# Two column halves instead of four column strips in the last matmuls of a decode layer, and its output stored as four rows

## The chip, the cores and the metric

The kernel runs on one core of a Trainium2 chip. The metric is the time of one execution on the device in microseconds (us), as the median of several runs. A separate execution is recorded by the hardware profiler; its span, from the first instruction to the last, is a little shorter than the time of that execution, because something lies around it.

A core has five engines that run side by side and meet through semaphores: TensorE (PE, the matmuls; its weight loads are shown apart as PEld), VectorE (DVE), ScalarE (ACT), GpSimd (POOL) and SyncE (SP), which here only issues DMAs. Matmuls write to PSUM, which has 128 partitions and eight banks of 512 fp32 columns; VectorE and ScalarE copy the results from there to SBUF, and DMAs move data between SBUF and the main memory (HBM).

## The reference

One decode step of a layer for B = 4 sequences with D = 512: attention over the last W = 4096 positions of a key and value cache (32 query heads, 8 key heads, 128 wide) in parallel with a gated feed-forward block (F = 1792), both on the same normalised input.

```python
xn  = layernorm(x)                                  # 4 x 512
q   = xn @ wq                                       # 32 heads of 128
p   = softmax(q @ k[last 4096].T * 128 ** -0.5)
att = (p @ v[last 4096]) @ wo
ffn = (silu(xn @ w_gate) * (xn @ w_up)) @ w_down
out = x + att + ffn                                 # 4 x 512, bf16
```

All tensors are bf16. The caches of the window are 64 MB, the weights some 13 MB.

## The kernel before

**The stream.** SP issues all the large loads from one queue, in the order of their use (`run_sync`, L227): W_q, the two feed-forward weights, then for each of the eight key heads 4 MB of keys and 4 MB of values into two buffers each, W_down, and W_o in five pieces (`ROWS`: rows j 0 to 15, 16 to 21, 22 to 28, 29 and 30, and 31), each piece with a semaphore of its own. Each load waits until the buffer that it fills is free.

**The start.** GpSimd writes constants (`run_gpsimd`, L190): identities, selection matrices, and `Dsh`, whose rows 64 to 67 hold 0 where a column belongs to a sequence and -BIG elsewhere. They come from a fill with zeros (L192), a fill of the four rows with -BIG (L209) and an `affine_select` (L211), which keeps an element where the compare holds and writes `fill` elsewhere. After the last constant it gives `s_const` (L220), for which PE (ahead of L461) and VectorE (ahead of L303) wait; then it fills P, guT and OP (L221 to L223). Meanwhile VectorE makes the layer norm, PE the projections with W_q (L467) and the feed-forward inputs (L481).

**The heads.** For each key head PE transposes the keys (L415), forms the scores (L424), the sums of exponentials (L515) and the product with the values (L433); VectorE and ScalarE copy, take maxima and exponentials in between. All that is not touched by the change.

**The end.** In `t_tail` (L554 on) PE gathers the heads' outputs, and accumulates in one PSUM bank, `part_ps`, the product with W_down (L566) and that with the first 22 rows of W_o (`EARLY`, L574). Row j stands for the 128 rows of W_o with index p * 32 + j; its weights on PE are `OP[:, j, :]`, 128 x 32. Each matmul there has 512 columns and goes to one of four strips of 32 partitions, so the four strips hold four partial sums of the whole output. VectorE copies partitions 0 to 63 of it to SBUF (L390), ScalarE partitions 64 to 127 (L274).

Then the order of the work turns round: in `acc_ps`, one bank, each strip n of 32 partitions holds the columns 128 n to 128 n + 127 of the output. First `fold`, a matrix of ones and zeros, sums the four partial sums (L579, fp32, one matmul a strip); then the last ten rows of W_o are added (L586, four matmuls of 128 columns for each row j, one a strip), each piece after a wait for its load. The last matmul gives `s_acc`; VectorE casts the 128 x 128 block to bf16 (L392) and gives `s_y`; SP stores it (L254) and waits for the store (L255). Only every eighth partition of a strip holds a sequence, so the store reads 16 partitions (`y_ap`), 256 bytes of each, into a pattern of three levels in HBM (`out_ap`). GpSimd waits for `s_acc` at its end (L225); nothing waits for that.

Of the kernel before, what the change touches and what calls it, by code (L numbers as in the profile page):

```python
# [3 lines left out]
BF16 = mybir.dt.bfloat16  # L4
FP32 = mybir.dt.float32
ALU = mybir.AluOpType
# [4 lines left out]
def bass_parallel_sum__sliding_block_cached__swiglu_ffn__decode_kernel(  # L11
# [12 lines left out]
    B, _, D = A_x.shape  # L24
# [11 lines left out]
    NC = D // 128  # L36
    NF = F // 128
    REP = HQ // HKV
# [6 lines left out]
    BIG = 1.0e30  # L45
# [3 lines left out]
    sb = nc.alloc_sbuf_tensor  # L49
# [6 lines left out]
    WO = KB[0][:].rearrange("p t d -> p (t d)").rearrange("p (j n) -> p j n", n=D)  # L56
# [22 lines left out]
    Dsh = sb("dsh", [128, CQ], BF16)  # L79
# [5 lines left out]
    OP = sb("oP", [128, 32, 32], BF16)  # L85
    guT = sb("guT", [128, NF, 32], BF16)
    part = sb("part", [128, D], FP32)
    y = sb("y_sb", [128, 128], BF16)

    ident = sb("ident", [128, 128], BF16)  # L90
    identf = sb("identf", [128, 128], FP32)
# [3 lines left out]
    fold = sb("fold", [128, 32], FP32)  # L95
# [6 lines left out]
    ps_S = [ps("ps_s%d" % s, [128, 512], FP32) for s in range(NB)]  # L102
# [14 lines left out]
    part_ps = ps_S[0]  # L117
    rt_ps = kt_ps[0][:, 0, :]
    op_ps = ps_S[1][:].rearrange("p (b q j) -> p b q j", b=B, q=4)
    acc_ps = ps_S[2]  # L120

    def sem(name):
        return nc.alloc_semaphore(name=name)
# [46 lines left out]
    s_acc = sem("s_acc")  # L170
    s_y = sem("s_y")

    x_ap = A_x.rearrange("b s d -> (b s) d")
    out_ap = out.rearrange("b s (n c) -> n (b s) c", n=NC)
    y_ap = y[0:128:8, :]
    wq_ap = A_wq.rearrange("(p c) n -> p c n", c=NC)
    wg_ap = B_w_gate.rearrange("(p c) n -> p c n", c=NC)
    wu_ap = B_w_up.rearrange("(p c) n -> p c n", c=NC)
# [11 lines left out]
    def run_gpsimd(eng):  # L190
        for t in (ident, identf, I4w, I48, Lsel, sel, mxd, Dsh):
            eng.memset(t[:], 0.0)  # L192
        eng.memset(ones[:], 1.0)
        eng.drain()
        eng.affine_select(ident[:], ident[:], pattern=[[-1, 128]], compare_op=ALU.not_equal,
                          fill=1.0, base=0, channel_multiplier=1).then_inc(s_c2, 1)
        eng.affine_select(identf[:], identf[:], pattern=[[-1, 128]], compare_op=ALU.not_equal,
                          fill=1.0, base=0, channel_multiplier=1)
        eng.drain()
        eng.memset(Lsel[0:16, :], 1.0)  # L200
        eng.drain()
        eng.memset(Lsel[32:48, :], 1.0)
        eng.drain()
        eng.affine_select(Lsel[64:68, :].rearrange("k (s b) -> k s b", b=B),
                          Lsel[64:68, :].rearrange("k (s b) -> k s b", b=B),
                          pattern=[[0, 32], [-1, B]], compare_op=ALU.not_equal,
                          fill=1.0, base=0, channel_multiplier=1)
        eng.drain()
        eng.memset(Dsh[64:68, :], -BIG)  # L209
        eng.drain()  # L210
        eng.affine_select(Dsh[64:68, :].rearrange("k (b h) -> k b h", b=B),  # L211
                          Dsh[64:68, :].rearrange("k (b h) -> k b h", b=B),
                          pattern=[[-1, B], [0, REP]], compare_op=ALU.not_equal,
                          fill=0.0, base=0, channel_multiplier=1)
        eng.drain()
        for q in range(4):
            v = sel[:].rearrange("k b (r h e) -> k b r h e", r=HKV, h=REP)[:, :, :, :, q]
            eng.affine_select(v, v, pattern=[[-REP, B], [-CQ, HKV], [-1, REP]], compare_op=ALU.not_equal,
                              fill=1.0, base=0, channel_multiplier=1)
        eng.drain().then_inc(s_const, 1)  # L220
        eng.memset(P[:], 1.0)  # L221
        eng.memset(guT[:], 0.0)
        eng.memset(OP[:], 0.0)  # L223
        eng.drain().then_inc(s_fill, 1)
        eng.wait_ge(s_acc, 1)  # L225

    def run_sync(eng):  # L227
        def load_k(r):
            if r >= 2:
                eng.wait_ge(s_tr[NCH - 1], r - 1)  # L230
            eng.dma_start(KB[r % 2][:].rearrange("p t d -> p (t d)"), kv_ap(A_k_cache, r)).then_inc(d_k[r % 2], 16)

        def load_v(r):
            if r:
                eng.wait_ge(s_pv, r)
            eng.dma_start(VB[r % 2][:].rearrange("p t d -> p (t d)"), kv_ap(A_v_cache, r)).then_inc(d_v[r % 2], 16)

        eng.dma_start(WQ[:], wq_ap).then_inc(d_v[1], 16)
        eng.dma_start(WG[:], wg_ap).then_inc(d_wg, 16)
        eng.dma_start(WU[:], wu_ap).then_inc(d_wu, 16)  # L240
        load_k(0)
        load_k(1)
        load_v(0)
        for r in range(2, HKV):
            load_k(r)
            load_v(r - 1)
        load_v(HKV - 1)
        eng.dma_start(WD, wd_ap).then_inc(d_wd, 16)  # L248
        for q, (a, b) in enumerate(ROWS):
            if q == 0:  # L250
                eng.wait_ge(s_tr[NCH - 1], HKV - 1)
            eng.dma_start(WO[:, a:b, :], wo_ap[:, a:b, :]).then_inc(d_wo[q], 16)  # L252
        eng.wait_ge(s_y, 1)
        eng.dma_start(out_ap, y_ap).then_inc(d_out, 16)  # L254
        eng.wait_ge(d_out, 16)  # L255

    def run_scalar(eng):
        eng.dma_start(X[:], x_ap).then_inc(d_x, 16)
        eng.wait_ge(s_var, 1)
        eng.activation(st_std[:], st_var[:], ACT.Sqrt).then_inc(s_std, 1)  # L260
        eng.wait_ge(s_q, 1)
        eng.copy(qs[:, 1, :], ps_S[1][:]).then_inc(s_qs, 1)
        eng.wait_ge(s_g, 1)
        eng.activation(ex, gate_ps[:], ACT.Exp, scale=-1.0).then_inc(s_ex, 1)
        with eng.Fori(0, HKV) as i:
            for n in BY_ACT:
                eng.wait_ge(s_tr[n], i + 1)
                eng.copy(KT[n % 8][:], kt_ps[n % 3]).then_inc(s_ev[n], 1)  # L268
            for q in range(NB):
                eng.wait_ge(s_sh[q], i + 1)  # L270
                eng.activation(P[:, q * TB:(q + 1) * TB, :], S_ps[q], ACT.Exp,  # L271
                               scale=SCALE).then_inc(s_xp[q], 1)
        eng.wait_ge(s_pt, 1)
        eng.copy(part[64:128, :], part_ps[64:128, :]).then_inc(s_ptc, 1)  # L274

    def run_vector(eng):
        me = bass.OrderedEngineSet([eng.engine])
# [111 lines left out]
        eng.wait_ge(s_pt, 1)  # L389
        eng.tensor_copy(part[0:64, :], part_ps[0:64, :]).then_inc(s_ptc, 1)  # L390
        eng.wait_ge(s_acc, 1)
        eng.tensor_copy(y[:], acc_ps[:, 0:128]).then_inc(s_y, 1)  # L392

    def run_tensor(eng):
        mm = eng.matmul
# [54 lines left out]
        with nc.body("t_head", valid_engines=me):  # L450
# [13 lines left out]
            for c in range(NC):  # L464
                for j in range(2):
                    for k in range(4):
                        last = mm(ps_S[j][32 * k:32 * k + 32, :], XnT[:, c, :],  # L467
                                  WQ[:, c, 512 * (4 * j + k):512 * (4 * j + k) + 512],
                                  start=(c == 0), stop=(c == NC - 1), skip_group_check=True)
# [26 lines left out]
        with nc.body("t_a_end", valid_engines=me):  # L496
            j = now(nx, 1, HKV)
# [3 lines left out]
        with nc.body("t_b_end", valid_engines=me):  # L501
            j = now(nx, 1, HKV)
# [3 lines left out]
        with nc.body("t_c_end", valid_engines=me):  # L506
            j = now(nx, 1, HKV)
# [3 lines left out]
        with nc.body("t_values", valid_engines=me):  # L511
            j = now(nx)
# [15 lines left out]
        with nc.body("t_p_end", valid_engines=me):  # L528
            j = now(nx)
# [24 lines left out]
        with nc.body("t_tail", valid_engines=me):  # L554
            eng.wait_ge(s_nm, LAST + 2)
            eng.transpose(rt_ps, OT[:, 1:, :].rearrange("p r c -> p (r c)"), ident[:]).then_inc(s_rt, 1)
            eng.wait_ge(s_rn, 1)
            for b in range(B):
                m = mm(op_ps[:, b].rearrange("p q j -> p (q j)"), sel[:, b, :], Rn[:], start=(b == 0), stop=True,
                       skip_group_check=True)  # L560
            m.then_inc(s_op, 1)
            eng.wait_ge(s_guT, 1)
            eng.wait_ge(d_wd, 16)
            for t in range(NF):
                k = (t + 1) % 4
                mm(part_ps[32 * k:32 * k + 32, :], guT[:, t, :], WD[:, t, :], start=(t < 3), stop=False,  # L566
                   skip_group_check=True)
            eng.wait_ge(s_opc, 1)
            for j in range(EARLY):
                for q, (a, b) in enumerate(ROWS):  # L570
                    if a == j:
                        eng.wait_ge(d_wo[q], 16)
                k = (j + 3) % 4
                m = mm(part_ps[32 * k:32 * k + 32, :], OP[:, j, :], WO[:, j, :], start=False,  # L574
                       stop=(j >= EARLY - 4), skip_group_check=True)
            m.then_inc(s_pt, 1)
            eng.wait_ge(s_ptc, 2)
            for n in range(NC):
                mm(acc_ps[32 * n:32 * n + 32, 0:128], fold[:], part[:, 128 * n:128 * n + 128],  # L579
                   start=True, stop=False, skip_group_check=True)  # L580
            for j in range(EARLY, 32):
                for q, (a, b) in enumerate(ROWS):
                    if a == j:
                        eng.wait_ge(d_wo[q], 16)
                for n in range(NC):
                    m = mm(acc_ps[32 * n:32 * n + 32, 0:128], OP[:, j, :], WO[:, j, 128 * n:128 * n + 128],  # L586
                           start=False, stop=(j == 31), skip_group_check=True)
            m.then_inc(s_acc, 1)
            step(seen, 1)
            eng.br_lt(seen, 1, on_true="t_tail", on_false="t_end").branch_hint(loc)  # L590
# [35 lines left out]
```

## Time and profile before

| | |
|---|---|
| time, median of 3 runs | 196.84 us (196.57 to 196.94) |
| the profiled execution's own time | 196.87 us |
| its span | 195.4 us |
| granted TensorE clock, mean over the span | 0.954 of full |
| busy: PE, VectorE, ScalarE, GpSimd | 155.1, 115.3, 68.9, 9.2 us |
| read from HBM | 81.01 MB, 415 GB/s over the span |

How to read the lines: times are in us unless they are marked ns. The page cuts the span in 40 equal slices and shows busy shares in tenths; the DMA row is the mean share of the core's 16 DMA engines. A line such as "L586 PE MATMUL ps_s<-kbuf,oP 128*32 128x128 bf16 x40" is a group: source line 586, on PE, writes the tile `ps_s` from `kbuf` and `oP`, weights of 128 x 32 and a moving operand of 128 x 128, forty times. In a timeline a row begins with its start and its duration, and the bracket at its end has the idle time of the engine before it and who ended that. The row of a stage has the stage, its length, the busy time of PE, PEld, VectorE, ScalarE and GpSimd with the number of instructions, then the granted clock, the DMA share and the GB/s. Tiles have several names: `part_ps` and `acc_ps` are both shown as `ps_s`, W_o lies in the first key buffer, `kbuf`, and W_down in `wg_sb`. Ends of matmuls are modelled, and records of matmuls overlap.

### The profile page before, as it was taken

How to read it: one execution, taken by the hardware profiler on the slowest of the kernel's cores; microseconds unless marked ns; L12 is line 12 of the kernel's file. 1: busy time of each engine (PE TensorE's matmuls, PEld its weight loads, DVE VectorE, ACT ScalarE, POOL GpSimd, SP SyncE). 2: the span in 40 equal slices, each digit the busy share in tenths (PEclk: the TensorE clock that was granted, in tenths of full speed). 3: DMA queues.
4: the chain of work that ended last, by engine and by line, in shares of the span. 5: the costliest groups of instructions: out<-in, count | busy, mean ns of one | idle time of the engine just before them, and what ended most of it. 6: DMA issues, size and time to landing. Idle time of an engine off the chain costs nothing.

```text
span 195.4 us, 6505 instructions
## 1 busy us (share of the span) xinstructions
PE 155.1 (79%) x2903; PEld 120.8 (62%) x2912; DVE 115.3 (59%) x220; ACT 68.9 (35%) x86; POOL 9.2 (5%) x27
## 2 busy tenths in 40 slices
PE   0038935997999899899989989998699879987653
PEld 0012105985788679778867968886598758955311
DVE  5642373666486766758676676867276747672501
ACT  2003100470447056444706634560447046603001
POOL 7820000000000000000000000000000000000000
PEclk9999996698799999999999999999889999999968
DMA  6999999999999999999999999999999999999991
GB/s 216 429 438 432 459 429 436 433 429 426 426 429 426 429 431 436 443 429 429 436 429 429 429 429 429 429 429 429 436 429 436 429 436 429 429 429 398 419 401 52
DMA packets 3633, 81.09 MB, mean 415 GB/s; under 512 B 424, under 2 KB 556, under 8 KB 940
## 3 DMA queue, kind: packets, MB, share of 16 engines
q1 hardware_dynamic: 3620, 81.01, 97.1%
q8 instruction: 4, 0.07, 0.1%
q14 instruction: 1, 0.01, 0.0%
q10 hardware_dynamic: 8, 0.00, 0.0%
HBM read 81.01 MB, written 0.00 MB: 415 GB/s over the span
## 4 chain that ended last, share of the span: by engine, by line
DMA 45%; PE 39%; ACT 7%; DVE 3%; issue 2%; SPq 2%; DVEq 0%
DMA kbuf<-in_A_k_cache_dram 28%; PE ps_kt L415 21%; DMA kbuf<-in_A_wo_dram 17%; PE ps_s L424 9%; ACT kT L268 7%; PE ps_o L433 6%; PE ps_s L532 2%; DVE mxb L339 2%; PE ps_kt L519 1%; PE ps_o L536 1%; SPq L252 1%; DVE mx L362 1%; DVE mxd L364 0%; DVE kT L335 0%; SPq L248 0%
## 5 line engine op out<-in xcount | busy, mean ns | idle before, releaser
L415 PE MATMUL ps_kt<-ident,kbuf 128*128 128x128 bf16 x1024 | 72.4, 227 | 9.5 <-DMA kbuf<-in_A_k_cache_dram 5.9
L415 PEld LDWEIGHTS ps_kt<-ident,kbuf 128*128 128x128 bf16 x1024 | 61.9, 102 | 16.8 <-ACT kT L268 6.4
L335 DVE COPY kT<-ps_kt 128x1024 bf16<-128x1024 bf16 x80 | 52.2, 687 | 20.3 <-PE ps_kt L415 19.5
L268 ACT COPY kT<-ps_kt 128x1024 bf16<-128x1024 bf16 x48 | 47.8, 1013 | 44.5 <-PE ps_kt L415 44.5
L271 ACT ACTIVATE p<-ps_s 128x512 bf16<-128x512 f32 x32 | 16.5, 604 | 46.1 <-PE ps_s L532 46.1
L339 DVE TENSOR_REDUCE mxb<-ps_s 128x16 f32<-128x512 f32 x32 | 22.1, 692 | 13.3 <-PE ps_s L424 11.6
L424 PE MATMUL ps_s<-qT,kT 128*128 x1024 | 29.4, 169 | 0.0
L424 PEld LDWEIGHTS ps_s<-qT,kT 128*128 128x128 bf16 x1024 | 27.8, 96 | 0.3
L433 PE MATMUL ps_o<-vbuf,p 128*32 128x256 bf16 x576 | 18.8, 287 | 1.3 <-DMA vbuf<-in_A_v_cache_dram 0.8
L433 PEld LDWEIGHTS ps_o<-vbuf,p 128*32 128x32 bf16 x576 | 16.1, 101 | 4.2 <-issue 3.4
L532 PE MATMUL ps_s<-dsh,lsel 128*128 128x512 bf16 x36 | 9.4, 381 | 0.0
L515 PE MATMUL ps_kt<-p,ones 128*128 128x512 bf16 x27 | 7.6, 379 | 0.9 <-ACT p L271 0.2
L467 PE MATMUL ps_s<-vbuf,xnT 128*32 128x512 bf16 x32 | 3.6, 629 | 5.0 <-DMA vbuf<-in_A_wq_dram 5.0
L519 PE MATMUL ps_kt<-identf,mxd 128*128 128x128 f32 x9 | 3.0, 328 | 5.3 <-DVEq L365 5.3
L343 DVE TENSOR_REDUCE dsum<-ps_kt 128x16 f32<-128x512 f32 x9 | 6.2, 692 | 1.5 <-PE ps_kt L515 1.3
L349 DVE TENSOR_TENSOR oT<-ps_o,rden 128x16 f32 (+1 forms) x9 | 1.6, 175 | 8.9 <-PE ps_o L536 8.9
L519 PEld LDWEIGHTS ps_kt<-identf,mxd 128*128 128x128 f32 x9 | 1.3, 140 | 8.4 <-DVEq L365 8.4
L536 PEld LDWEIGHTS ps_o<-fold,o 128*128 128x128 f32 x36 | 5.4, 190 | 1.3
L347 DVE COPY o<-ps_o 128x256 f32<-128x256 f32 x9 | 3.8, 425 | 3.8 <-PE ps_o L433 3.2
L574 PE MATMUL ps_s<-kbuf,oP 128*32 128x512 bf16 x22 | 2.8, 623 | 3.8 <-DMA kbuf<-in_A_wo_dram 3.8
L457 PE MATMUL ps_s<-ident,xn 4*128 4x4 bf16 x4 | 0.3, 166 | 6.6 <-DVE xn L297 6.6
L274 ACT COPY part<-ps_s 64x512 f32<-64x512 f32 x1 | 0.6, 580 | 13.4 <-PE ps_s L574 13.4
(92 smaller groups left out, 71.7 us busy)
## 6 DMA issues: line engine op xcount, KB each, us to landing
kbuf<-in_A_k_cache_dram SPq DMA_DIRECT2D x8, 4096.0 KB, 24.3
vbuf<-in_A_v_cache_dram SPq DMA_DIRECT2D x8, 4096.0 KB, 26.2
vbuf<-in_A_wq_dram SPq DMA_DIRECT2D x1, 4096.0 KB, 12.1
kbuf<-in_A_wo_dram SPq DMA_DIRECT2D x1, 2048.0 KB, 29.9
wg_sb<-in_B_w_gate_dram SPq DMA_DIRECT2D x1, 1792.0 KB, 16.0
wu_sb<-in_B_w_up_dram SPq DMA_DIRECT2D x1, 1792.0 KB, 19.8
wg_sb<-in_B_w_down_dram SPq DMA_DIRECT2D x1, 1792.0 KB, 25.6
kbuf<-in_A_wo_dram SPq DMA_DIRECT2D x1, 896.0 KB, 33.0
```

The costliest lines, as they stand in the source:

```text
L268: eng.copy(KT[n % 8][:], kt_ps[n % 3]).then_inc(s_ev[n], 1)
L271: eng.activation(P[:, q * TB:(q + 1) * TB, :], S_ps[q], ACT.Exp, scale=SCALE).then_inc(s_xp[q], 1)
L335: eng.tensor_copy(KT[n % 8][:], kt_ps[n % 3]).then_inc(s_ev[n], 1)
L339: eng.tensor_reduce(mxb[:, q, :], S_ps[q].rearrange("p t c -> p c t"), AX.X, ALU.max)
L343: eng.tensor_reduce(dsum[:], dn_ps[:].rearrange("p (t c) -> p c t", c=CQ), AX.X, ALU.add)
L415: last = eng.transpose(kt_ps[n % 3][:, k, :], KB[g][:, 8 * n + k, :], ident[:])
L424: last = mm(S_ps[q][:, 8 * (n % 4) + k, :], KT[n % 8][:, k, :], QT[:, bass.ds(j, 1), :, :].rearrange("p o b h -> p (o b h)"), start=(n % 4 ...
L433: last = mm(o4_ps[32 * k:32 * k + 32, :], P[:, 2 * u:2 * u + 2, :].rearrange("p t c -> p (t c)"), VB[e][:, 2 * u:2 * u + 2, :].rearrange(" ...
L515: last = mm(dn_ps[:], ones[:], P[:, q * TB:(q + 1) * TB, :].rearrange("p t c -> p (t c)"), start=(q == 0), stop=(q == NB - 1))
L519: eng.transpose(mx_ps, mxd[:], identf[:]).then_inc(s_mt, 1)
L532: mm(S_ps[q], Lsel[:], bc(Dsh[:], TB), start=False, stop=True, skip_group_check=True).then_inc(s_sh[q], 1)
L536: last = mm(ot_ps, o4[:, 128 * e:128 * e + 128], fold[:, 16 * e:16 * e + 16], start=(e == 0), stop=(e == 1), skip_group_check=True)
```

## The change

The four strips of 128 columns become two halves of 256 columns: columns 0 to 255 in partitions 0 to 31 of one bank, columns 256 to 511 in partitions 32 to 63 of another. So the fold is two matmuls instead of four, and each of the last ten rows of W_o two instead of four, of twice the length. VectorE casts the first half and ScalarE the second, both onto partitions 0 to 31 of `y`, which is now 32 x 512; SP waits for both and stores four partitions of 1 KB each. Apart from that, GpSimd no longer fills the four rows of `Dsh` with -BIG: the select now keeps the zeros and writes -BIG where the compare fails.

```diff
--- before.py
+++ after.py
@@ -85,7 +85,7 @@
     OP = sb("oP", [128, 32, 32], BF16)
     guT = sb("guT", [128, NF, 32], BF16)
     part = sb("part", [128, D], FP32)
-    y = sb("y_sb", [128, 128], BF16)
+    y = sb("y_sb", [32, D], BF16)
 
     ident = sb("ident", [128, 128], BF16)
     identf = sb("identf", [128, 128], FP32)
@@ -117,7 +117,8 @@
     part_ps = ps_S[0]
     rt_ps = kt_ps[0][:, 0, :]
     op_ps = ps_S[1][:].rearrange("p (b q j) -> p b q j", b=B, q=4)
-    acc_ps = ps_S[2]
+
+    acc_ps = [ps_S[2][0:32, 0:D // 2], ps_S[3][32:64, 0:D // 2]]
 
     def sem(name):
         return nc.alloc_semaphore(name=name)
@@ -171,8 +172,8 @@
     s_y = sem("s_y")
 
     x_ap = A_x.rearrange("b s d -> (b s) d")
-    out_ap = out.rearrange("b s (n c) -> n (b s) c", n=NC)
-    y_ap = y[0:128:8, :]
+    out_ap = out.rearrange("b s d -> (b s) d")
+    y_ap = y[0:32:8, :]
     wq_ap = A_wq.rearrange("(p c) n -> p c n", c=NC)
     wg_ap = B_w_gate.rearrange("(p c) n -> p c n", c=NC)
     wu_ap = B_w_up.rearrange("(p c) n -> p c n", c=NC)
@@ -206,12 +207,10 @@
                           pattern=[[0, 32], [-1, B]], compare_op=ALU.not_equal,
                           fill=1.0, base=0, channel_multiplier=1)
         eng.drain()
-        eng.memset(Dsh[64:68, :], -BIG)
-        eng.drain()
         eng.affine_select(Dsh[64:68, :].rearrange("k (b h) -> k b h", b=B),
                           Dsh[64:68, :].rearrange("k (b h) -> k b h", b=B),
-                          pattern=[[-1, B], [0, REP]], compare_op=ALU.not_equal,
-                          fill=0.0, base=0, channel_multiplier=1)
+                          pattern=[[-1, B], [0, REP]], compare_op=ALU.is_equal,
+                          fill=-BIG, base=0, channel_multiplier=1)
         eng.drain()
         for q in range(4):
             v = sel[:].rearrange("k b (r h e) -> k b r h e", r=HKV, h=REP)[:, :, :, :, q]
@@ -250,7 +249,7 @@
             if q == 0:
                 eng.wait_ge(s_tr[NCH - 1], HKV - 1)
             eng.dma_start(WO[:, a:b, :], wo_ap[:, a:b, :]).then_inc(d_wo[q], 16)
-        eng.wait_ge(s_y, 1)
+        eng.wait_ge(s_y, 2)
         eng.dma_start(out_ap, y_ap).then_inc(d_out, 16)
         eng.wait_ge(d_out, 16)
 
@@ -272,6 +271,8 @@
                                scale=SCALE).then_inc(s_xp[q], 1)
         eng.wait_ge(s_pt, 1)
         eng.copy(part[64:128, :], part_ps[64:128, :]).then_inc(s_ptc, 1)
+        eng.wait_ge(s_acc, 1)
+        eng.copy(y[:, D // 2:], acc_ps[1]).then_inc(s_y, 1)
 
     def run_vector(eng):
         me = bass.OrderedEngineSet([eng.engine])
@@ -389,7 +390,7 @@
         eng.wait_ge(s_pt, 1)
         eng.tensor_copy(part[0:64, :], part_ps[0:64, :]).then_inc(s_ptc, 1)
         eng.wait_ge(s_acc, 1)
-        eng.tensor_copy(y[:], acc_ps[:, 0:128]).then_inc(s_y, 1)
+        eng.tensor_copy(y[:, 0:D // 2], acc_ps[0]).then_inc(s_y, 1)
 
     def run_tensor(eng):
         mm = eng.matmul
@@ -575,15 +576,14 @@
                        stop=(j >= EARLY - 4), skip_group_check=True)
             m.then_inc(s_pt, 1)
             eng.wait_ge(s_ptc, 2)
-            for n in range(NC):
-                mm(acc_ps[32 * n:32 * n + 32, 0:128], fold[:], part[:, 128 * n:128 * n + 128],
-                   start=True, stop=False, skip_group_check=True)
+            for h in range(2):
+                mm(acc_ps[h], fold[:], part[:, 256 * h:256 * h + 256], start=True, stop=False, skip_group_check=True)
             for j in range(EARLY, 32):
                 for q, (a, b) in enumerate(ROWS):
                     if a == j:
                         eng.wait_ge(d_wo[q], 16)
-                for n in range(NC):
-                    m = mm(acc_ps[32 * n:32 * n + 32, 0:128], OP[:, j, :], WO[:, j, 128 * n:128 * n + 128],
+                for h in range(2):
+                    m = mm(acc_ps[h], OP[:, j, :], WO[:, j, 256 * h:256 * h + 256],
                            start=False, stop=(j == 31), skip_group_check=True)
             m.then_inc(s_acc, 1)
             step(seen, 1)
```

## The prediction

> **What bounds the kernel now.** I read the span and the DMA row of the page first, then the chain of waits cut to the end, then the timeline of the last eight microseconds.
>
> ```profile
> span 195.4 us, 6505 instructions
> ...
> DMA  6999999999999999999999999999999999999991
> ```
>
> The DMA row stands at 9 from the second slice to the last but one: the loads stream without a break and the rest hides under them. A change pays only if it shortens the stream or what is left after its last byte. This change does nothing to the stream, so only the end counts. The chain of waits there:
>
> ```profile
> 159.36 33.26 DMA kbuf<-in_A_wo_dram
> ...
> 192.97 0.27 PE ps_s L586 x4
> ```
>
> The pieces of W_o land, and after the last one come four matmuls (0.27), a cast and the store. The same end as a timeline (start, duration, engine; in brackets the idle time before and who ended it):
>
> ```profile
> 190.85 0.58 ACT L274 COPY part<-ps_s 64x512 f32<-64x512 f32 x1 [13.41 <-PE ps_s L574]
> 190.85 0.68 DVE L390 COPY part<-ps_s 64x512 f32<-64x512 f32 x1 [5.55 <-PE ps_s L574]
> 191.58 0.16 PEld L579 LDWEIGHTS ps_s<-part,fold 128*32 128x32 f32 x8 [1.69 <-DVE part L390]
> 191.59 0.42 PE L579 MATMUL ps_s<-part,fold 128*32 128x128 f32 x8 [0.78 <-DVE part L390]
> 191.96 0.40 PEld L586 LDWEIGHTS ps_s<-kbuf,oP 128*32 128x32 bf16 x28 [0.22 <-DMA kbuf<-in_A_wo_dram]
> 191.96 1.25 PE L586 MATMUL ps_s<-kbuf,oP 128*32 128x128 bf16 x40
> 192.66 0.12 PEld L586 LDWEIGHTS ps_s<-kbuf,oP 128*32 128x32 bf16 x8 [0.30 <-DMA kbuf<-in_A_wo_dram]
> 192.97 0.10 PEld L586 LDWEIGHTS ps_s<-kbuf,oP 128*32 128x32 bf16 x4 [0.19 <-DMA kbuf<-in_A_wo_dram]
> 193.26 0.29 DVE L392 CAST y_sb<-ps_s 128x128 bf16<-128x128 f32 x1 [1.73 <-PE ps_s L586]
> 193.58 0.69 SPq L254 DMA_DIRECT2D out_dram<-y_sb  x1
> ```
>
> Three times PE waits for W_o: rows 22 to 28 start at 191.96, 29 and 30 at 192.66, 31 at 192.97. So in front of the last landing PE has idle time (0.22, 0.30 and 0.19), which the change can spend before it costs anything.
>
> **GpSimd: nothing.** The -BIG fill and its drain go; the select keeps its size.
>
> ```profile
> 4.96 0.10 POOL L209 MEMSET dsh<- 4x16 bf16 x1
> 5.19 0.21 POOL L211 TENSOR_SCALAR_AFFINE_SELECT dsh<-dsh 4x16 bf16<-4x16 bf16 x1
> ...
> 13.05 0.16 PEld L467 LDWEIGHTS ps_s<-vbuf,xnT 128*32 128x32 bf16 x8 [5.02 <-issue]
> ...
> 16.73 0.58 ACT L262 CAST kT<-ps_s 128x512 bf16<-128x512 f32 x1 [11.08 <-PE ps_s L467]
> 16.73 0.17 DVE L308 COPY mask<-ps_o 128x16 f32<-128x16 f32 x1 [4.79 <-PE ps_s L467]
> ```
>
> The later select starts 0.23 sooner (5.19 - 4.96), and so do the constants and P's fill behind it. Who waits for them sits idle anyway: PE 5.02 us for W_q, VectorE 4.79 us for PE. If the compare with the other sense were dearer (no row shows it), it would have to cost over 4 us to be seen.
>
> **PE: +0.10.** Before, each row j is four matmuls of 128 columns in four strips of 32 PSUM partitions; after, two of 256 columns in two strips and two banks. The paces, first from the timeline, then from each line's own view (shortest, median and longest record in ns):
>
> ```profile
> 191.96 0.57 PE L586 MATMUL ps_s<-kbuf,oP 128*32 128x128 bf16 x28
> ```
>
> ```profile
> 178.75 1.93 PE L433 MATMUL ps_o<-vbuf,p 128*32 128x256 bf16 x64 [0.75 <-DMA vbuf<-in_A_v_cache_dram]
> ```
>
> ```profile
> L586 PE MATMUL ps_s<-kbuf,oP x40: 219/219/230, 192.0 to 193.0; 128*32 128x128 bf16 x40
> ```
>
> ```profile
> L433 PE MATMUL ps_o<-vbuf,p x576: 269/273/421, 48.0 to 180.4; 128*32 128x256 bf16 x192
> ```
>
> ```profile
> L579 PE MATMUL ps_s<-part,fold x8: 272/285/297, 191.6 to 191.7; 128*32 128x128 f32 x8
> ```
>
> Strips stream side by side. Rows 22 to 28 are seven sets of four: (0.57 - 0.22) / 6 = 0.058 a set of 128 columns. The 64 of L433 are sixteen sets: (1.93 - 0.27) / 15 = 0.11 a set of 256 columns. So the length of one strip's matmul sets the pace, not their number, and a row j goes from 0.058 to 0.11, if two strips run beside each other as four do (rival 2 if not).
>
> The fold (L579) goes first: four fp32 matmuls, recorded as eight, two rounds of four strips. An fp32 record of 128 columns takes 272 at its shortest, as a bf16 one of 256 columns does (269), so I take fp32 as streaming twice the columns: a round of 256 columns takes what 512 bf16 columns would, 2 x 0.11 = 0.22. From above: the round now takes 0.42 - 0.28 = 0.14, and twice that is 0.28. I take 0.22: in the short rounds of before, the second set of weight loads may have set the pace (eight loads, 0.16 in all), and under 0.22 it hides.
>
> Then: fold from 191.59 to 192.03; rows 22 to 28, 7 x 0.11, to 192.80; 29 and 30, whose weights landed by 192.66, to 193.02; row 31 starts at 193.02 and not at 192.97. That is +0.05, as the idle time in front is used up. Its record is 273 instead of 219: +0.05. Together +0.10. Bounds: +0.04 if row 31 still starts with its landing; +0.22 with fold rounds of 0.28, which put row 31 at 193.14.
>
> **The casts: +0.13.** One cast of 128 columns on all 128 partitions becomes two of 256 columns on 32 partitions, side by side.
>
> ```profile
> L347 DVE COPY o<-ps_o x9: 424/425/425, 51.4 to 180.7; 128x256 f32<-128x256 f32 x9
> ```
>
> An engine's time goes by columns: VectorE takes 0.29 for 128 and 0.425 for 256, so its half is 0.13 longer than the whole was. ScalarE's 512 columns took 0.58, on 128 partitions (L262, above) as on 64 (L274), so its 256 lie below that: 0.58 is the bound, +0.29 instead of +0.13. VectorE drops by 0.26 from 512 columns to 256 (0.68 to 0.425), so I expect about 0.35 of ScalarE, and VectorE's cast ends last. In the fence above ScalarE and VectorE both leave a long wait at 190.85, so the second engine doesn't start late. That ScalarE reads partitions 32 to 63 and writes 0 to 31 is in no row; I take nothing for it, and the 0.58 covers it. Nothing is queued behind the new wait on ScalarE; the store on SP waits for the later cast.
>
> **The store: -0.19.** Sixteen rows of 256 B in a three-level pattern become four rows of 1 KB in a plain one.
>
> ```profile
> L258 ACTq DMA_DIRECT2D x_sb<-in_A_x_dram x1: 557/557/557, 0.8 to 0.8; - x1
> ```
>
> ```profile
> L238 SPq DMA_DIRECT2D vbuf<-in_A_wq_dram x1: 386/386/386, 0.8 to 0.8; - x1
> ```
>
> ```profile
> L236 SPq DMA_DIRECT2D vbuf<-in_A_v_cache_dram x8: 534/535/657, 3.5 to 156.7; - x8
> ```
>
> ```profile
> SPq L255 <- DMA out_dram<-y_sb: 1.0, 1, 1.0
> ```
>
> ```profile
> GB/s 0 0 0 0 0 0 0 0 0 0 34 34 68 68 34 68 34 69 1 68 0 35 0 34 0 1 0 0 0 0 0 0 0 0 0 0 0 0 0 0
> ```
>
> The load of x is the store's mirror: four rows of 1 KB, plain. Its issue takes 0.56 where the store's takes 0.69; on SP the plain W_q takes 0.39 and the three-level V 0.535, a like step of 0.14. So -0.14. Bounds: 0, as x is a load on another queue, and -0.30 by W_q's 0.39. The last row is the DMA traffic from 194.80 to 195.10 in forty slices: the store's packets lie in slices 11 to 24, 194.875 to 194.98, about 0.1. A quarter of the packets, each four times as long, side by side, should need about half of it: -0.05 (0 to -0.1). Between the end of the issue (194.28) and the first packet lie 0.60, and from the last packet to the end of SP's wait (194.28 + 1.0) lie 0.3; I leave both.
>
> [...]
>
> **Sum.** +0.10 + 0.13 - 0.14 - 0.05 = +0.04 us. The profiled execution took 196.87, its span 195.4 and 1.47 around it; that is 0.03 over the median of 196.84. So 196.88 to 196.91: I say 196.9. All lows together (0.04 + 0.13 - 0.30 - 0.1) give -0.23, all highs (0.22 + 0.29) +0.51. About 0.2%, or 0.39 us, is what a measurement of this kernel can tell from no change.
>
> **Rival 1, slower: the clock in the tail.**
>
> ```profile
> 136.30:139.73 3.43, 1.61 (x20) 0.92 (x10) 0.80 (x3) 2.07 (x4) 0.00 (x0) 1.00 0.89 382
> 139.73:143.14 3.41, 3.37 (x32) 3.37 (x33) 1.98 (x3) 0.00 (x0) 0.00 (x0) 0.50 1.07 461
> 184.02:187.43 3.41, 0.16 (x2) 0.00 (x0) 1.13 (x3) 0.00 (x0) 0.00 (x0) 1.00 0.96 403
> 187.43:190.85 3.42, 2.82 (x22) 0.65 (x22) 0.00 (x1) 0.00 (x1) 0.00 (x0) 0.51 0.97 388
> 190.85:194.26 3.41, 1.48 (x48) 0.78 (x48) 0.97 (x2) 0.58 (x1) 0.00 (x0) 0.99 0.12 44
> ```
>
> These stages are cut where the granted clock steps (the column before the last two). After a window in which PE, waiting for W_o, is busy for 0.16 us, the clock halves at 187.43 for 3.41 us and is full again at 190.85, just ahead of the tail. At 0.51 of the clock the same streaming takes about twice as long. If in other executions the half stretch ends at E after 191.59, the tail after the change, 0.44 + 1.10 of streaming with hardly a gap, ends (E - 191.59) / 2 later; the tail before, with 0.14 rounds, 0.058 sets and 0.7 of idle time, absorbs nearly all of it. It decides once E passes 191.6. With E at 192.4 the cost is +0.4, so 197.3; at 193.3, +0.85. For it: half stretches followed windows with 0.16 and with 1.61 us of PE work, and the steps lie on a grid (139.73 + 14 x 3.41 = 187.47) that no stage of the kernel has, so a stretch from 188.2 to 191.6, or from 189.9 to 193.3, is plausible elsewhere. Against it: in the one execution shown the step falls clear of the tail, and the median over runs moves only if most of them are hit. [...]
>
> **Rival 2, slower: two strips in two banks take turns.** Every row above has its strips in one bank. In turns, a row j takes 0.22 and the fold 0.88: 191.59 + 0.88 + 9 x 0.22 = 194.45 for the start of row 31's set instead of 192.97. With 0.11 until its second half starts and the other terms (0.05 + 0.13 - 0.19) that is +1.6: 198.5. It decides as soon as a set takes longer than 0.11. Nothing in the trace speaks for it.
>
> **Rival 3, faster: the store's latency shrinks too.** The traffic from 1.60 to 1.90, again in forty slices:
>
> ```profile
> GB/s 0 0 0 0 0 0 0 0 0 0 0 0 0 0 0 0 0 0 0 137 137 0 0 137 0 1 1 137 1 4369 0 4369 1 4369 4369 0 0 0 4369 4369
> ```
>
> x's first packet is in slice 20, at 1.74, 0.94 after its issue starts; the store's comes 1.29 after (193.58 to 194.875). At x's figure the store gains 0.35 instead of 0.14, and with 0.25 of the 0.3 behind the packets gone too the sum is -0.42: 196.4. Against it: on SP the plain W_q, issued from 0.8 to 1.19, has its first packets (the large figures) in slice 30, at 1.82, 0.63 after its issue ends, and the store's 0.60 is no longer than that.
>
> **How the numbers follow.** The forecast gets 0.68, rival 1 0.20, rival 2 0.04, rival 3 0.08. Slower by over 0.2%: rival 2, about half of rival 1, 0.02 of the forecast's highs: 0.16. Faster: rival 3's larger half and 0.02 of the forecast: 0.07. The rest, 0.77, is no change. The range takes in the forecast's bounds, most of rivals 1 and 3: 196.45 to 197.4.
>
> **What would show it.** In the profile after: the fold at about 0.5 instead of 0.42; L586's sets 0.11 apart, row 31's start within 0.1 of its landing; both casts under 0.45, ScalarE ending first; the issue of the store near 0.56; the wait behind it near 1.0. Sets 0.22 apart at full clock would be rival 2, at half clock rival 1; an issue that stays at 0.69 would make the change slower by 0.14 than said; a wait below 0.8 would be rival 3.

## The result and the profile after

The kernel after takes 198.35 us (198.28 to 198.36) where the kernel before takes 196.84 (196.57 to 196.94): the ratio is 1.0081, with a 95% interval of 1.0069 to 1.0093. It is slower by 1.5 us. The forecast was 196.9 and a range up to 197.4.

The chain of waits of the profile after, cut to the end (start, duration, what):

```profile
156.29 31.27 DMA kbuf<-in_A_wo_dram
187.56 0.14 issue
187.69 2.85 PE ps_s L575 x22
190.54 0.02 issue
190.57 0.69 DVE part L391
191.26 0.04 issue
191.31 1.07 PE ps_s L580 x4
192.38 2.15 PE ps_s L586 x20
194.53 0.02 issue
194.55 0.41 DVE y_sb L393
```

Before, the chain went from a landing of W_o to the last four matmuls. Now the last DMA in it is the first piece of W_o, landed at 187.56, and from the copies at 190.57 on it is TensorE that sets the end: the pieces for the last ten rows are there before it wants them (by the trace they land at 191.64, 192.35 and 192.66; the matmuls of row 22 start at 192.16, behind the fold, and those of row 31 at 194.08). Lines have moved a little: L575 was L574, L580 was L579, L391 was L390, L393 was L392, L253 was L254; the last ten rows are L586 in both. The timeline of the same stretch:

```profile
191.31 1.07 PE L580 MATMUL ps_s<-part,fold 128*32 128x256 f32 x4 [0.78 <-DVE part L391]
191.74 0.16 PEld L586 LDWEIGHTS ps_s<-kbuf,oP 128*32 128x32 bf16 x2 [0.24 <-DMA kbuf<-in_A_wo_dram]
192.16 2.35 PE L586 MATMUL ps_s<-kbuf,oP 128*32 128x256 bf16 x20
192.16 1.86 PEld L586 LDWEIGHTS ps_s<-kbuf,oP 128*32 128x32 bf16 x18 [0.27 <-issue]
194.55 0.36 ACT L275 CAST y_sb<-ps_s 32x256 bf16<-32x256 f32 x1 [3.40 <-PE ps_s L586]
194.55 0.41 DVE L393 CAST y_sb<-ps_s 32x256 bf16<-32x256 f32 x1 [3.30 <-PE ps_s L586]
194.99 0.75 SPq L253 DMA_DIRECT2D out_dram<-y_sb  x1
```

Four steps hold the difference between the spans, which the traces have to the nanosecond as 195.36 and 196.82. The last ten rows start at 192.16 instead of 191.96: +0.20, although the fold itself started 0.28 earlier, as W_o came earlier in this execution (its last piece landed at 192.66 instead of 192.93). From there to the casts it takes 2.39 instead of 1.30: +1.09. From the start of the casts to the store's issue it takes 0.44 instead of 0.32: +0.12. From the issue to the end of the span it is 1.83 instead of 1.78: +0.06 before rounding. The sum is +1.47, which with the roundings is the 1.46 between the spans.

So it is TensorE, and the records of the last ten rows say why (shortest, median and longest in ns, from the line's own view):

```profile
L586 PE MATMUL ps_s<-kbuf,oP x20: 421/421/421, 192.2 to 194.1; 128*32 128x256 bf16 x20
```

The same shape took 273 in L433 before. The sets of two start (2.35 - 0.42) / 9 = 0.214 apart, not 0.11. The two strips still run side by side: the trace has the two starts of the first set at 192.162 and 192.169 and those of the second at 192.375 and 192.382, so the two of a set start together. What has changed is the clock. Here are the stages of the profile after, cut where its clock may step (stage, length, busy time of PE, PEld, VectorE, ScalarE, GpSimd, granted clock, DMA share, GB/s):

```profile
182.37:185.79 3.42, 1.49 (x19) 0.56 (x18) 2.05 (x5) 0.00 (x0) 0.00 (x0) 1.00 0.93 396
185.79:189.20 3.41, 1.50 (x16) 0.54 (x16) 0.00 (x0) 0.00 (x0) 0.00 (x0) 0.50 1.03 424
189.20:192.61 3.41, 2.63 (x20) 0.81 (x18) 0.68 (x1) 0.58 (x1) 0.00 (x0) 0.50 0.52 197
192.61:196.02 3.41, 1.90 (x18) 1.08 (x14) 0.41 (x1) 0.36 (x1) 0.00 (x0) 0.50 0.00 0
```

In the profile before, the half clock lasted for one window, 187.51 to 190.93, and the tail had the full clock. (The prediction's stages are cut 0.08 before these steps, which is why they read 0.51 and 0.99.) Here it lasts from 185.79 to the end.

### The profile page after: what moved, and what is told of

It is laid out like the page before. It is cut to its first block, busy times and chain, and to the rows that moved or that the text cites. A ratio compares the mean times of both kernels' runs of the same rounds, so it can differ in the third digit from the quotient of the medians.

```text
span 196.8 us, 6465 instructions
## 1 busy us (share of the span) xinstructions
PE 156.6 (80%) x2888; PEld 121.7 (62%) x2888; DVE 115.4 (59%) x220; ACT 69.2 (35%) x87; POOL 8.8 (4%) x26
## 4 chain that ended last, share of the span: by engine, by line
DMA 45%; PE 41%; ACT 7%; DVE 3%; issue 1%; SPq 1%; DVEq 0%
DMA kbuf<-in_A_k_cache_dram 29%; PE ps_kt L416 20%; DMA kbuf<-in_A_wo_dram 16%; PE ps_s L425 9%; ACT kT L267 7%; PE ps_o L434 5%; PE ps_s L533 2%; DVE mxb L340 2%; PE ps_s L575 1%; PE ps_s L586 1%; PE ps_kt L520 1%; PE ps_o L537 1%; DVE mx L363 1%; PE ps_s L580 1%; DVE mxd L365 0%
## 5 line engine op out<-in xcount | busy, mean ns | idle before, releaser
L434 PE MATMUL ps_o<-vbuf,p 128*32 128x256 bf16 x576 | 17.4, 273 | 0.6
L434 PEld LDWEIGHTS ps_o<-vbuf,p 128*32 128x32 bf16 x576 | 15.0, 97 | 2.2 <-issue 1.8
L516 PE MATMUL ps_kt<-p,ones 128*128 128x512 bf16 x36 | 9.7, 378 | 0.2
L575 PE MATMUL ps_s<-kbuf,oP 128*32 128x512 bf16 x22 | 2.8, 624 | 3.5 <-DMA kbuf<-in_A_wo_dram 3.5
L468 PEld LDWEIGHTS ps_s<-vbuf,xnT 128*32 128x32 bf16 x32 | 1.3, 140 | 7.0 <-issue 7.0
L533 PEld LDWEIGHTS ps_s<-dsh,lsel 128*128 128x128 bf16 x36 | 2.8, 97 | 4.1 <-issue 1.9
```

The costliest lines, as they stand in the source:

```text
L434: last = mm(o4_ps[32 * k:32 * k + 32, :], P[:, 2 * u:2 * u + 2, :].rearrange("p t c -> p (t c)"), VB[e][:, 2 * u:2 * u + 2, :].rearrange(" ...
L516: last = mm(dn_ps[:], ones[:], P[:, q * TB:(q + 1) * TB, :].rearrange("p t c -> p (t c)"), start=(q == 0), stop=(q == NB - 1))
L533: mm(S_ps[q], Lsel[:], bc(Dsh[:], TB), start=False, stop=True, skip_group_check=True).then_inc(s_sh[q], 1)
```

## The experiments

**Theory A.** TensorE idles for 3.51 us while it waits for W_o (the wait ahead of L575 in the profile after), the clock halves (0.50 from 185.79 on) and stays there through the tail. With four strips of 128 columns the tail's streaming is so short that the half clock hides behind the landings; with two strips of 256 columns it is twice as long and doesn't. **Theory B:** two strips, or two banks, take turns whatever the clock. **Theory C:** the casts by two engines and the store carry most of it.

**after_warm: the idle time filled.** To the kernel after, fifteen matmuls are added, whose result nobody reads:

```diff
+            for w in range(15):
+                mm(ps_kt[1][:], ident[:], P[:, 0:TB, :].rearrange("p t c -> p (t c)"), start=True, stop=True)
             eng.wait_ge(s_opc, 1)
             for j in range(EARLY):
```

> The kernel after, plus fifteen matmuls of 512 columns on the full array into an unused PSUM bank, put between the product with W_down and the wait for the first piece of W_o, to fill the 3.5 us in which TensorE otherwise idles; their result is never read. Theory A (the granted clock is at half in the whole tail because TensorE idled before it, and two strips make the stream twice as long, so the half clock is paid in full): the clock column is 1.0 from 184 to the end, the sets of two matmuls start 0.11 apart, row 31 starts within 0.1 of its landing, and the time falls by about 1.3 to 197.0 (196.8 to 197.3). Theory B (two strips, or two banks, take turns whatever the clock): sets stay 0.21 apart and the time stays at 198.3.

Measured: 196.86 (196.61 to 197.33), ratio to the kernel before 0.9999 (0.9986 to 1.0013). The whole 1.5 us is gone. Its tail, as a timeline and then as stages:

```profile
191.10 0.62 PE L582 MATMUL ps_s<-part,fold 128*32 128x256 f32 x4 [0.78 <-DVE part L391]
191.90 1.11 PEld L588 LDWEIGHTS ps_s<-kbuf,oP 128*32 128x32 bf16 x20 [0.66 <-DMA kbuf<-in_A_wo_dram]
191.90 1.30 PE L588 MATMUL ps_s<-kbuf,oP 128*32 128x256 bf16 x20 [0.17 <-DMA kbuf<-in_A_wo_dram]
193.24 0.36 ACT L275 CAST y_sb<-ps_s 32x256 bf16<-32x256 f32 x1 [2.30 <-PE ps_s L588]
193.24 0.41 DVE L393 CAST y_sb<-ps_s 32x256 bf16<-32x256 f32 x1 [2.20 <-PE ps_s L588]
193.68 0.75 SPq L253 DMA_DIRECT2D out_dram<-y_sb  x1
```

```profile
185.91:189.32 3.41, 2.93 (x25) 1.07 (x23) 0.00 (x0) 0.00 (x0) 0.00 (x0) 1.00 1.00 412
189.32:192.74 3.42, 2.07 (x26) 1.00 (x28) 0.68 (x1) 0.58 (x1) 0.00 (x0) 1.00 0.50 193
192.74:196.15 3.41, 0.46 (x8) 0.13 (x4) 0.41 (x1) 0.36 (x1) 0.00 (x0) 1.00 0.00 1
```

```profile
L588 PE MATMUL ps_s<-kbuf,oP x20: 272/273/283, 191.9 to 192.9; 128*32 128x256 bf16 x20
```

At full clock the same twenty matmuls take 1.30, the sets are (1.30 - 0.27) / 9 = 0.114 apart, and TensorE waits for W_o again (0.66 and 0.17 of idle time put down to the DMA). From the first of the ten rows to the casts it takes 1.34, where the kernel before took 1.30. Theory B is out: two strips in two banks run side by side at this clock too.

Not all of the gain lies in these rows. The first 22 rows of W_o now ran at full clock as well, so the fold starts at 191.10 instead of 191.31. From the fold's start to the casts it takes 2.14 instead of 3.24.

**before_warm: the same fill in the kernel before.** The same two lines, at the same place.

> The kernel before with the same fifteen filling matmuls. Theory A: its tail waits for W_o, not for TensorE, so a full clock buys nothing: 196.8 (within 0.2). Theory B says the same. If it gains 0.3 or more, the half clock cost the kernel before as well, and theory A overstates what the change alone did.

Measured: 196.90 (196.52 to 197.81), ratio 1.0001 (0.9982 to 1.0021). The fill by itself gains nothing, so what it gave the kernel after is what that had lost.

**after_onebank: both halves in one bank.**

```diff
-    acc_ps = [ps_S[2][0:32, 0:D // 2], ps_S[3][32:64, 0:D // 2]]
+    acc_ps = [ps_S[2][0:32, 0:D // 2], ps_S[2][32:64, 0:D // 2]]
```

> The kernel after with both halves in one PSUM bank (still partitions 0 to 31 and 32 to 63). Theory A: nothing changes: at half clock sets 0.21 apart and 198.3. Theory B in its form with the banks: the two strips now stream side by side as the four did before, sets about half as far apart at the same clock, and 197 or less.

Measured: 198.39 (two executions), ratio 1.008 (1.0058 to 1.0103). Line and stage of its profile:

```profile
192.31 2.35 PE L586 MATMUL ps_s<-kbuf,oP 128*32 128x256 bf16 x20
```

```profile
192.39:195.80 3.41, 2.27 (x22) 1.30 (x18) 0.41 (x1) 0.36 (x1) 0.00 (x0) 0.50 0.00 0
```

The same 2.35 at the same half clock. There the second bank costs nothing and gains nothing; no run shows one bank at full clock.

**strips_rows: only cast and store changed.** The kernel before, with its four strips, but cast into the four rows strip by strip, and stored as the kernel after does (first ScalarE, then VectorE, then SP):

```diff
+        eng.wait_ge(s_acc, 1)
+        for n in (2, 3):
+            eng.copy(y[:, 128 * n:128 * n + 128], acc_ps[32 * n:32 * n + 32, 0:128]).then_inc(s_y, 1)
...
-        eng.tensor_copy(y[:], acc_ps[:, 0:128]).then_inc(s_y, 1)
+        for n in (0, 1):
+            eng.tensor_copy(y[:, 128 * n:128 * n + 128], acc_ps[32 * n:32 * n + 32, 0:128]).then_inc(s_y, 1)
...
-        eng.wait_ge(s_y, 1)
+        eng.wait_ge(s_y, 4)
```

> The kernel before (four strips of 128 columns, GpSimd unchanged), but cast strip by strip, two strips on VectorE and two on ScalarE, into the four rows of the kernel after, and stored as four rows of 1 KB. So only cast and store are changed. Theory A: TensorE's part is that of before; two casts of 128 columns one behind the other take about 0.55 instead of 0.29, and the store's issue 0.75 instead of 0.69: 196.84 + 0.25 + 0.05 = 197.15 (197.0 to 197.4). Theory C (casts by two engines and the store carry most of the 1.5): 198 or more.

Measured: 196.98 (196.76 to 197.38), ratio 1.0016 (1.0005 to 1.0026). That is just under the 197.0 at which theory A's range began, and theory C is out. This profile shows something more, for its tail happened to run at half clock, with four strips:

```profile
191.59 0.66 PE L583 MATMUL ps_s<-part,fold 128*32 128x128 f32 x8 [0.78 <-DVE part L393]
191.97 1.13 PEld L590 LDWEIGHTS ps_s<-kbuf,oP 128*32 128x32 bf16 x40 [0.18 <-DMA kbuf<-in_A_wo_dram]
192.02 1.29 PE L590 MATMUL ps_s<-kbuf,oP 128*32 128x128 bf16 x40
193.35 0.54 ACT L277 CAST y_sb<-ps_s 32x128 bf16<-32x128 f32 x2 [1.92 <-PE ps_s L590]
193.35 0.59 DVE L396 CAST y_sb<-ps_s 32x128 bf16<-32x128 f32 x2 [1.82 <-PE ps_s L590]
193.97 0.74 SPq L254 DMA_DIRECT2D out_dram<-y_sb  x1
```

```profile
192.10:195.51 3.41, 1.21 (x44) 0.95 (x36) 0.56 (x2) 0.52 (x2) 0.00 (x0) 0.50 0.02 5
```

From the fold's start to the casts it takes 1.76 (191.59 to 193.35), where the kernel before, at full clock and with the last row waiting at 192.97, took 1.67 (191.59 to 193.26). The profile of before_actstore, further down, has four strips and a tail at half clock too (records of 314 ns in L586 where the profile before has 219), and takes 1.77 (191.90 to 193.67). So for four strips the half clock costs about 0.1, and for two it costs 1.1 or more (3.24 against the 2.14 of after_warm). This is theory A's second half, shown without touching the clock.

**after_again: the kernel after once more.** Nothing is edited.

> The kernel after, unchanged, for more executions. Theory A with the clock at half in the tail as the rule: every execution 198.2 to 198.5. Theory A', as rival 1 of the prediction had it (the end of the half stretch differs between executions, many are spared): a spread from 197.0 to 198.4.

Measured: a median of 198.38, ratio 1.0059 (1.0031 to 1.0087), but in two groups: 196.94, 197.00 and 197.22, and five from 198.36 to 198.58. The first expectation falls, and so does the second: nothing lies between the groups. The mean granted clock of the first three is 0.956 to 0.965, that of the five 0.938 to 0.949. So 1.5 us is the cost in the second group, in which all four executions of the result lie, and not in every execution; the first group lies about 0.3 above the 196.73 that the kernel before took beside it. The profile is of the second group; its two windows around the tail:

```profile
186.44:189.85 3.41, 1.94 (x20) 0.66 (x22) 0.00 (x0) 0.00 (x0) 0.00 (x0) 0.50 0.99 404
189.85:193.27 3.42, 2.64 (x20) 1.02 (x16) 0.68 (x1) 0.58 (x1) 0.00 (x0) 0.50 0.36 135
```

**after_warm8 and after_thin: less fill.** The same lines with `range(8)`; and with fifteen, but on one strip each:

```diff
+            for w in range(15):
+                mm(ps_kt[1][0:32, :], ident[:, 0:32], P[:, 0:TB, :].rearrange("p t c -> p (t c)"), start=True, stop=True)
```

> The kernel after with eight filling matmuls instead of fifteen (about 1.7 us of the 3.5 filled). If a stretch without any work of about 3.4 us is what halves the clock, half of the filling is enough: 196.9. If the share of busy time in a window of 3.41 us decides, executions differ or stay slow: 197.2 to 198.3.

> The kernel after with fifteen filling matmuls of which each uses one strip only (weights of 128 x 32 instead of 128 x 128), so TensorE is busy as long, 3.2 us, with a quarter of the array. If busy time is what keeps the clock: 196.9, as with the full fill. If the part of the array that works counts too: half clock and 198.3, and then the two strips of the tail themselves would help to keep the clock down.

Measured: with eight, 197.33 (196.69 to 198.58), ratio 1.0037 (1.0009 to 1.0064), spread over the whole distance; the five up to 197.11 have a mean granted clock of 0.972 to 0.974, the five from 197.55 on 0.946 to 0.964. So half a fill still seems to let the clock fall in some executions (the profiled one, of 196.93, kept it). With one strip, 196.98 (196.66 to 198.07), ratio 1.0017 (0.9997 to 1.0036): six of ten, up to 197.06, as with the full fill (mean granted clock 0.956 to 0.973), though each filling matmul has weights of 128 x 32 only; but four of ten lie from 197.34 on (0.962 to 0.964). Its profile, of an execution of 198.04, shows how:

```profile
185.30:188.72 3.42, 2.66 (x22) 1.12 (x24) 0.15 (x1) 0.00 (x0) 0.00 (x0) 1.00 0.97 402
188.72:192.13 3.41, 1.72 (x23) 0.29 (x14) 0.68 (x1) 0.58 (x1) 0.00 (x0) 1.00 0.69 270
192.13:195.54 3.41, 2.29 (x20) 1.32 (x20) 0.41 (x1) 0.36 (x1) 0.00 (x0) 0.50 0.01 4
```

The fill kept the clock up to 192.13; then came a window with only 1.72 us of work, the waits for W_o among it, and half clock for the ten rows alone: 2.35 from 192.10 to the casts at 194.45, where after_warm took 1.34. So half clock followed here on a window that wasn't idle. Whether a share of the window decides, and which, isn't shown, as a window with 1.66 was followed by full clock in the profile with eight:

```profile
187.23:190.65 3.42, 1.66 (x22) 0.50 (x22) 0.21 (x1) 0.21 (x1) 0.00 (x0) 1.00 0.98 392
190.65:194.06 3.41, 1.94 (x24) 1.03 (x24) 0.89 (x2) 0.74 (x2) 0.00 (x0) 1.00 0.13 50
```

Whether one strip is a weaker fill than four, ten executions don't settle.

**gpsimd_only: GpSimd's edit alone.**

```diff
-        eng.memset(Dsh[64:68, :], -BIG)
-        eng.drain()
...
-                          pattern=[[-1, B], [0, REP]], compare_op=ALU.not_equal,
-                          fill=0.0, base=0, channel_multiplier=1)
+                          pattern=[[-1, B], [0, REP]], compare_op=ALU.is_equal,
+                          fill=-BIG, base=0, channel_multiplier=1)
```

> The kernel before with only GpSimd's edit (no fill with -BIG, the select with the other sense). All theories: the constants come some 0.2 us sooner and nobody is held up by them: within 0.2 of 196.8.

Measured: 196.79 (196.61 to 196.98), ratio 1.0004 (0.9994 to 1.0014). Nothing, as expected.

**warm_actstore and before_actstore: the store from ScalarE's queue.** In after_warm and in the kernel before, SP's last three lines move to the end of ScalarE's program (with a wait for 1 in the kernel before):

```diff
+        eng.wait_ge(s_y, 2)
+        eng.dma_start(out_ap, y_ap).then_inc(d_out, 16)
+        eng.wait_ge(d_out, 16)
```

> The kernel after with the fifteen filling matmuls, and with the store issued from ScalarE's queue, behind its own cast, instead of from SP's. If the queue was what made the load of x (four rows of 1 KB) issue in 0.56 where the store took 0.75 on SP: an issue of about 0.56 and 0.2 less than with the fill alone, 196.65. If it is the direction, from SBUF to HBM, or the length of the program behind it: 0.75 and no gain, 196.85.

> The kernel before with its store of sixteen rows issued from ScalarE's queue. If the queue decides: an issue of about 0.5 to 0.6 instead of 0.69, and 196.6 to 196.7. If not: 0.69 and 196.8.

Measured: 196.99 (196.91 to 197.25), ratio 1.0014 (1.0005 to 1.0023), and 196.96 (196.75 to 197.16), ratio 1.0004 (0.9990 to 1.0017). The issues, of four rows and of sixteen:

```profile
193.73 0.70 ACTq L274 DMA_DIRECT2D out_dram<-y_sb  x1
```

```profile
193.99 0.63 ACTq L273 DMA_DIRECT2D out_dram<-y_sb  x1
```

The queue is worth 0.05 or 0.06 of the issue, and nothing of the time: with four rows it is 1.83 from the start of the issue to the end of the span on either queue. On both queues four rows issue slower than sixteen, by 0.05 to 0.07, and both slower than x's 0.56. What makes a store's issue longer than a load's of the same shape stays open.

## Why the prediction was wrong

**What bounds the kernel:** right for the kernel before. It was also said that in front of the last landing PE had idle time to spend: true, 0.7 us, but at half clock the change needs over twice that.

**GpSimd, nothing:** right (1.0004, 0.9994 to 1.0014).

**PE, +0.10:** this is the step that failed. Its working holds at full clock: sets 0.114 apart for 0.11, records of 273 for 273, and in after_warm the ten rows take 0.04 more than before, at the lower of the bounds of 0.04 and 0.22. (The +0.05 for a late start of row 31 isn't tested there, since the fold starts at 191.10 and not at 191.59.) But every pace in it was read off stages with the full clock, and the one profile shown had the full clock in the tail by the luck of its windows: of the four profiles with four strips and no fill, strips_rows and before_actstore have the half clock there (0.50, and records of 314 for 219). In the kernel after at half clock a set takes 0.214 and the stretch from the fold's start to the casts 194.55 - 191.31 = 3.24 instead of 193.26 - 191.59 = 1.67. That is +1.57 where the sum has +0.10: TensorE's streaming ends last, and no wait for row 31's landing is left on the path.

**The casts, +0.13:** right. VectorE took 0.41 and ScalarE 0.36, for 0.425 and 0.35; cast to issue is 0.44 instead of 0.32, +0.12. Reading partitions 32 to 63 and writing 0 to 31 cost ScalarE nothing that shows.

**The store, -0.19:** wrong. The issue got longer, 0.75 instead of 0.69, where -0.14 was taken from the load of x; from the start of the issue to the end of the span it is 1.83 after and 1.78 before, so the store cost 0.06 more and not 0.19 less. All of it is the issue: from its end to the end of the span it is 1.08 in both, so sixteen rows of 256 B end as soon after their issue as four of 1 KB.

**The sum:** at full clock the terms measured are +0.04, +0.12 and +0.06: +0.22, not +0.04. The ratio of after_warm, up to 1.0013 (+0.26 us), just takes that in.

**Rival 1, the clock in the tail, given 0.20 and 197.3:** this is what happened; its mechanism was right and its price and its chance were wrong. It let the half stretch be one window long, so that it ended by 193.3 and cost at most 0.85. Its rule, a delay of half the time spent at half clock, fits: half of 3.24 is 1.62, where 1.57 was measured. The windows show what it missed. The profile before already has a half stretch of two windows, early in the heads, where a window with 2.58 us of PE work was followed by another:

```profile
30.50:33.90 3.40, 2.58 (x25) 2.59 (x26) 1.35 (x2) 0.00 (x0) 0.00 (x0) 0.50 0.94 405
33.90:37.30 3.40, 3.40 (x35) 3.40 (x33) 2.06 (x4) 1.01 (x1) 0.00 (x0) 0.50 1.08 458
```

Ahead of the tail, a window with 2.82 us of work led from half clock back to full in the profile before (187.51 to 190.93), and one with 2.83 in that of gpsimd_only, which has the four strips; its two windows:

```profile
188.06:191.47 3.41, 2.83 (x22) 0.66 (x22) 0.48 (x1) 0.48 (x1) 0.00 (x0) 0.50 0.82 326
191.47:194.88 3.41, 1.49 (x48) 0.78 (x48) 0.49 (x2) 0.10 (x1) 0.00 (x0) 1.00 0.07 24
```

Windows with 2.63 (after) and 2.64 (strips_rows, after_again) did not. So ahead of the tail the clock came back only after windows that held nearly the whole of the 2.85 us of L574: they started 0.48 (the profile before) and 0.06 us (gpsimd_only) ahead of it. In the five profiles with another grid and no fill (after, after_again, after_onebank, strips_rows, before_actstore) the tail stayed at half clock to its end, and then the whole stream doubles (sets of two 0.214 apart for 0.114). So the chance was not 0.2: nine of the first twelve executions of the kernel after, and both of after_onebank, were above 198.2. The text weighed the grid, but asked only where a half stretch of one window would fall, not what it takes to end it; the rows were there, as it quotes the window of 2.82 before the full clock.

**Rival 2, two strips take turns, 198.5:** its time came true and its mechanism did not: the paces of 0.214 at half clock and 0.114 at full are those of strips side by side. Had only the pace been read, without the clock column and the starts within a set, the sets 0.21 apart would have looked like its proof.

**Rival 3, the store's latency:** refuted with the store.

One measure puts all twelve profiles on one scale, whenever W_o came: the time from the landing of its last piece to the start of the casts. With four strips it is 0.34 at full clock (before, before_warm, gpsimd_only) and 0.41 at half clock (strips_rows, before_actstore). With two it is 0.37 at full clock (after_warm, after_warm8, warm_actstore), 1.89 or 1.90 at half clock (after, after_again, after_onebank), and 1.38 where the ten rows alone ran at half clock (after_thin).

Theory A stands: the fill removes the loss without touching a matmul of the tail, two strips at the same half clock lose what four do not, and the executions of one kernel fall into the two groups. That the groups of after_again are two phases of the windows is argued from the profiles; no profile shows an execution of its first group.

## What to carry to other kernels

A narrower use of TensorE can be nearly free at full clock (+0.04 here) and dear at half clock (+1.1 or more): where a stage follows a wait of TensorE, price its streaming at half clock too, whatever the one profile shows, and ask what it takes for the clock to come back. Splitting an output over strips so that one matmul is short is worth keeping in such a tail even if fewer, longer matmuls look equal. Fifteen matmuls in the wait, whose result nobody reads, kept the clock at 1.00 in the profile of after_warm (198.35 to 196.86 us), but they only made good what the stage would lose; here no version was faster than the kernel before.

## What the runs showed of the hardware

- The clock steps on a grid of 3.41 us: in the profile before, the steps at 30.50 and 187.51 lie 46 times 3.413 apart, in that after those at 28.78 and 185.79. Its place differs between executions: its steps were at 187.51 (before), 185.79 (after), 186.44 (after_again) and 188.06 (gpsimd_only), for kernels whose work up to there is the same but for GpSimd's edit. Half clock followed on a window without PE work (gpsimd_only, 184.65 to 188.06), but also on windows with 1.49 (after) and 1.72 us of work (after_thin), while those with 2.07 (after_warm) and 1.66 (after_warm8) were followed by full clock. There is no sharp threshold in these sums of modelled records: among the heads, in the profile before, a window with 2.09 (44.15 to 47.56) was followed by half clock too.
- Coming back took more work than staying: in the profiles before and after and the windows read of the other runs, windows at half clock with up to 2.64 of 3.41 us of work (strips_rows and after_again) were followed by another, and those with 2.82 (before, 187.51 to 190.93) or more by full clock.
- A plain store of four rows of 1 KB issued in 0.75 on SP and 0.70 on ScalarE's queue, a three-level one of sixteen rows of 256 B in 0.69 and 0.63, and the load of x, four rows of 1 KB, in 0.56. From the end of the issue to the end of the span it took 1.08 on SP and 1.13 on ScalarE's queue, whatever the rows.
